# Other digits for how feed-forward pieces and inversion steps are laid between the blocks of an RWKV-7 attention kernel

## The chip, the core and the metric

The kernel runs on one core of a Trainium2 chip: TensorE (in the profile PE for its matmuls and PEld for its weight loads), VectorE (DVE), ScalarE (ACT), GpSimd (POOL), and SyncE (SP), which issues most DMAs. The metric is the device time of one execution in microseconds, and the time of a kernel is the median of its runs.

## The reference: what is computed

```python
# attention, B=4, H=8, S=768, D=40; state is (B, H, D, D)
for t in range(S):
    y[:, :, t] = einsum('bhd,bhde->bhe', rt, state)
    Sa = einsum('bhde,bhe->bhd', state, at)
    state = state * wt[:, :, None, :] - einsum('bhd,bhe->bhde', Sa, bt) \
            + einsum('bhd,bhe->bhde', vt, kt)
x = y.transpose(0, 2, 1, 3).reshape(3072, 320)
# feed-forward, 320 -> 2048 -> 320
h = x @ w_in
out = (h * clip(h + 3, 0, 6) / 6) @ w_out
```

The recurrence over time is sequential; the feed-forward of a token needs only that token's row of `y`.

## The kernel before, in words

**Units.** The attention is cut into chunks of 64 steps. A unit is one chunk of two batches, all heads at once; there are 24 units (`NK`), four (`NU`) to a group of 128 steps. For a unit, `prepare` (L579) does what needs no state: `W` and `gam` (products of the decays, two scans at L599 and L610), `A`, `B`, `K`, `factor` (turning and scaling the inputs), `F` (the products that make up the matrix to invert), `E` and `EV`. `step` (L882) does the rest: `RT` and `VT` (turn), `R` (L921), `C` and `H` (scores, L562, masked on VectorE at L575), `U` and `UT` (L961, L981), `rS` (L997) and `y`, which also updates the state (matmuls L1043, VectorE L1050 and L1055). `move` and `move2` bring `y` into the layout of the feed-forward by DMA.

**Inversion.** Once for a group, when `F` of its last unit is there, `invert` (L778) inverts 32 triangular 32x32 blocks per row of lanes on VectorE: a transpose (L783), then 30 pairs of one multiply (L803) and one add (L809), then two transposes `tb` (L812) and `tt` (L817), then copies to `tinv` on ScalarE and GpSimd. It is a generator: one call of `aside(1)` (L1254) issues the instructions up to its next `yield`. The first call issues the transpose, the second and third nothing, each of the next sixty one multiply or one add, the 64th `tb`, the 65th `tt`. `third_block` (L828) then does the off-diagonal parts on TensorE (L838 and L861, copied out by ScalarE at L846 and L871). It needs `tb` and `tt`.

**Feed-forward.** For each unit there are two jobs. `expand` (L1165) multiplies by 1024 columns of `w_in` into two PSUM banks (`h`, two buffers, both used by each job); when the last product is in, `results` (L1183) takes them out: ScalarE relu (L1186), then VectorE minimum and product (L1187), which frees the banks. `contract` (L1204) multiplies by `w_out` (`o`). `feed_forward` (L1142) runs expand of a job, then contract of the job before it, then expand of the next, and so on: an expand therefore waits until L1187 of the expand before it has run. The stream is a generator too; one `next(stream)` is a *piece*. From unit 7 on, a job has eight pieces: four of expand (four matmuls of 128x128 each) and four of contract (two matmuls with 320 columns each). The eight short matmuls of expand (64 rows, `win2`) are no piece then: they are issued inside the next block's products, and if all four expand pieces are issued by then, `results` follows them at once, else it follows the fourth.

**Order.** The order is written out by hand, engine by engine, as Python emits it; each engine works its list in that order. Units 4 to 23 take four *blocks* each, 80 blocks in all (0 to 79 below, `m` in the code). Block `m` of unit `i` has m = 4(i-4)+j. `a_block(m)` (L1483) issues the stages that fall into that block: those of the unit's own `step` (`RT` and `VT` in its first block, `R`, `C` and `S` in the second, `U`, `UT` and `rS` in the third, `H` in the fourth, `y` in the fifth, so the twenty groups of L1043 stand in blocks 4, 8, ... 80, and the moves in the sixth) and those of the units being prepared ahead. It does so in two parts: the stages of units whose preparation began at a multiple of four blocks with the unit's own, and the stages of the others; after block 14 the second part is always empty. In the first two blocks of the first two units of a group, `block` (L1368) adds the third blocks, L838 in the first of them and L861 in the second. Feed-forward pieces are put between the two parts and after the second part (and the third block) by `feed` (L1506):

```python
def feed(n, inversion):
    for _ in range(n):
        next(stream)
        aside(inversion)
```

with `GAPS` (L1515, pieces per block) and `INVERSION` (L1516, calls of `aside` after each piece of that block), one digit for each block. Before the third block of a group's first unit, `aside(3 * L)` issues what is left of the inversion.

```python
for j in range(BLOCKS):
    amount, inversion = int(GAPS[m]), int(INVERSION[m])
    parts = a_block(m)
    next(parts)                       # first part
    ...                               # first = how many pieces come here
    feed(first, inversion)
    for _ in parts: pass              # second part
    if third_here: ...                # aside(3 * L) once a group, then block(i, j)
    feed(amount - first, inversion)
    m += 1
```

After block 79 the stream runs out whatever is left.

## Time and profile before

| | |
|---|---|
| runs of the kernel before, median | 793.05 us |
| lowest to highest of its 3 runs | 792.87 to 794.69 us |
| the profiled execution | 790.23 us |
| its span in the profile | 788.5 us |
| mean granted TensorE clock in it | 0.954 |
| blocks 0 to 79 | from 194 us on; L1043 of block 16 starts at 314.10 us, of block 32 at 427.60 us, of block 40 at 470.88 us |

The profile shows one execution, a little below the lowest of the three timed runs. In a timeline row the first number is the start in us, the second how long the group was busy, and in brackets stands how long the engine sat idle before it and which instruction ended that. Each fp32 matmul of 128x128 or of 320 columns has two records, so one expand piece is 8 records of L1171 (`h`), one contract piece 4 records of L1212 (`o`), and the short matmuls of a job are 16 records of L1171. In the table of waits stand the engine and line that waited, the line that ended the wait, the sum in us, how often, and the longest.

### The profile page before, as it was taken

Reading aid. Unit: us, or ns where it says so; the run is one execution under the profiler, and the core shown is the slowest. Engines: PE = TensorE matmul, PEld = TensorE weight load, DVE = VectorE, ACT = ScalarE, POOL = GpSimd, SP = SyncE. Lnnn points to the kernel's source line nnn. Section 1 sums busy time; section 2 is a strip of 40 time slices with the busy share of each in tenths; the row PEclk is TensorE's granted clock in tenths of the full one; section 3 lists DMA queues with packets and bytes.
Section 4 is the critical chain, followed back from the end, with each engine's and each line's share of the span. In section 5 each row is a group of like instructions: output and inputs, shape, how many; then the busy total and the mean of one; then the engine's idle time right before and its main releaser. Section 6 shows DMA issues by size and latency. Waiting matters only on the chain.

```text
span 788.5 us, 32736 instructions
## 1 busy us (share of the span) xinstructions
PE 724.5 (92%) x14464; PEld 611.9 (78%) x14464; DVE 508.5 (64%) x1020; ACT 299.0 (38%) x634; POOL 168.2 (21%) x319
## 2 busy tenths in 40 slices
PE   5826888999899997999999999999999999999998
PEld 3725677878778776788888788888888888888886
DVE  8898799688445798555798556997535892233110
ACT  2345673232544442542424454134543233422111
POOL 7503002421222412122203222113222100000000
PEclk9855689999999998999999999999999999999999
DMA  9682384320244421334331344323332201211000
GB/s 124 113 205 62 91 210 75 63 48 12 50 73 76 89 54 27 77 77 90 60 63 36 74 82 87 67 47 68 69 69 57 43 17 38 47 38 29 20 9 17
DMA packets 195698, 52.34 MB, mean 66 GB/s; under 512 B 179428, under 2 KB 194276, under 8 KB 195556
## 3 DMA queue, kind: packets, MB, share of 16 engines
q1 hardware_dynamic: 187932, 46.88, 30.2%
q10 hardware_dynamic: 7624, 3.36, 1.7%
q8 instruction: 114, 1.87, 1.0%
q14 instruction: 28, 0.23, 0.1%
HBM read 38.67 MB, written 3.93 MB: 54 GB/s over the span
## 4 chain that ended last, share of the span: by engine, by line
PE 72%; DVE 15%; issue 4%; ACT 3%; DMA 2%; SPq 1%; POOL 1%; ACTq 1%; DVEq 0%; POOLq 0%
PE h L1171 26%; PE o L1212 23%; PE pair L562 4%; PE pair L1043 3%; DVE prod L803 2%; DVE x L809 2%; PE pair L534 2%; PE pair L961 2%; PE one L524 1%; DVE wm L610 1%; PE pair L997 1%; DVE prods L599 1%; PE pair L861 1%; PE pair L981 1%; PE pair L921 1%
## 5 line engine op out<-in xcount | busy, mean ns | idle before, releaser
L1171 PE MATMUL h<-xt,win 128*128 128x128 f32 (+1 forms) x2304 | 250.2, 284 | 5.9 <-DVE gt L1187 5.8
L1171 PEld LDWEIGHTS h<-xt,win 128*128 128x128 f32 (+1 forms) x2304 | 231.6, 193 | 22.4 <-DVE gt L1187 6.9
L1212 PE MATMUL o<-wout,gt 128*128 128x320 f32 x768 | 228.3, 441 | 0.0
L1212 PEld LDWEIGHTS o<-wout,gt 128*128 128x128 f32 x768 | 138.6, 190 | 51.7
L1187 DVE SCALAR_TENSOR_TENSOR gt<-gt,h 128x512 f32<-128x512 f32 x96 | 61.6, 682 | 105.1 <-ACT gt L1186 105.1
L1186 ACT ACTIVATE gt<-h,three 128x512 f32<-128x512 f32 x96 | 61.4, 684 | 133.1 <-PE h L1171 113.9
L803 DVE TENSOR_TENSOR prod<-x 128x30 f32<-128x30 f32 (+9 forms) x180 | 66.6, 370 | 6.4 <-POOL x L788 1.3
L809 DVE TENSOR_TENSOR x<-x,prod 128x30 f32<-128x30 f32 (+9 forms) x180 | 64.7, 360 | 5.9
L575 DVE COPY_PREDICATED store<-mask,pair 128x512 f32<-128x512 int32 x40 | 29.2, 729 | 54.5 <-PE pair L562 41.0
L1051 POOL TENSOR_TENSOR yg<-ys,gam 128x512 f32<-128x512 f32 x20 | 25.4, 1272 | 150.0 <-DVE ys L1050 145.1
L723 POOL TENSOR_TENSOR KBt<-K,rgt 128x320 f32<-128x320 f32 x19 | 16.7, 881 | 145.5 <-ACT rgt L712 140.3
L599 DVE TENSOR_TENSOR_SCAN prods<-wm,start 128x528 f32<-128x528 f32 x24 | 33.4, 1398 | 11.2 <-ACT wm L596 10.8
L1043 PE MATMUL pair<-store,KBt 64*64 64x104 f32 x1280 | 32.6, 250 | 0.6 <-ACT F L693 0.6
L610 DVE TENSOR_TENSOR_SCAN wm<-wm,start 128x528 f32<-128x528 f32 x24 | 31.0, 1293 | 0.8
L757 ACT ACTIVATE EV<-pair 64x320 f32<-64x320 f32 x46 | 19.8, 431 | 29.9 <-PE pair L752 26.3
L1043 PEld LDWEIGHTS pair<-store,KBt 64*64 64x64 f32 x1280 | 29.2, 133 | 1.5 <-ACT F L693 0.7
L642 POOL TENSOR_TENSOR at<-at,gam 128x512 f32<-128x512 f32 x12 | 15.3, 1271 | 65.8 <-DVE at L478 65.8
L950 ACT ACTIVATE S<-pair 128x512 f32<-128x512 f32 x16 | 9.6, 597 | 47.9 <-DVE store L575 27.1
L871 ACT ACTIVATE tinv<-pair 32x256 f32<-32x256 f32 x48 | 17.9, 374 | 21.4 <-PE pair L861 20.8
L783 DVE STREAM_TRANSPOSE fb<-F 128x1024 f32<-128x1024 f32 x6 | 12.9, 2155 | 18.8 <-ACT F L693 16.8
L1230 ACT ACTIVATE ob<-o 128x320 f32<-128x320 f32 x22 | 9.6, 437 | 40.6 <-issue 25.9
L932 ACT ACTIVATE VT<-pair 128x512 f32<-128x512 f32 x21 | 12.5, 598 | 32.6 <-PE pair L562 18.2
(298 smaller groups left out, 1064.5 us busy)
## 6 DMA issues: line engine op xcount, KB each, us to landing
R<-in_r_dram SPq DMA_DIRECT2D x156, 40.0 KB
A<-in_a_dram SPq DMA_DIRECT2D x61, 80.0 KB
V<-in_v_dram SPq DMA_DIRECT2D x96, 40.0 KB
out_dram<-ob SPq DMA_DIRECT2D x47, 80.0 KB
B<-in_b_dram SPq DMA_DIRECT2D x42, 80.0 KB
store<-V SPq DMA_DIRECT2D x20, 160.0 KB
W<-in_w_dram SPq DMA_DIRECT2D x37, 80.0 KB
K<-in_k_dram SPq DMA_DIRECT2D x37, 80.0 KB
```

Of the source, the lines that this page charges most:

```text
L562: nc.tensor.matmul(out=o[i][half(q), n, :], lhsT=lhs[half(i, D), n ^ (2 * q * swap), half(q)], rhs=rhs[half(i, D), n ^ (2 * q * back), hal ...
L575: nc.vector.copy_predicated(out=x[:, :, 0:BL].rearrange("p (h i) t -> p i h t", i=2), mask=mask8, data=o[2])
L599: nc.vector.tensor_tensor_scan(out=prods[:].rearrange("p r m i -> p (r m i)"), data0=wm[:, 0:SCAN], data1=start[:], initial=0.0, op0=ALU.m ...
L610: nc.vector.tensor_tensor_scan(out=back, data0=back, data1=start[:], initial=0.0, op0=ALU.mult, op1=ALU.add)
L803: nc.vector.tensor_tensor(out=pv, in0=_ap(x[:], (i + 1) * L + i, [[L, n], [0, i]]), in1=_ap(x[:], i * L, [[0, n], [1, i]]), op=ALU.mult,)
L809: nc.vector.tensor_tensor(out=rest, in0=rest, in1=pv, op=ALU.add)
L1043: nc.tensor.matmul(out=y[q][half(s), pr, :], lhsT=o[name][half(q), h * D:h * D + SLOT], rhs=m[name][half(q), x, :], start=(name == "K" and ...
L1051: nc.gpsimd.tensor_tensor(out=yg[:], in0=m["ys"][:].rearrange("p r q t -> p r (q t)"), in1=o["G"][:], op=ALU.mult)
L1171: nc.tensor.matmul(out=hp[c][:, i, :], lhsT=lhsT, rhs=rhs, start=(begun[c] == 0), stop=(begun[c] == 3 * NQ - 1))
L1186: nc.scalar.activation(out=gt[:], in_=hp[c][:], func=AF.Relu, bias=three[:], scale=1.0)
L1187: nc.vector.scalar_tensor_tensor(out=gt[:], in0=gt[:], scalar=6.0, in1=hp[c][:], op0=ALU.min, op1=ALU.mult)
L1212: nc.tensor.matmul(out=op[:], lhsT=gts[c][:, n, :], rhs=wout[:, c * HJ + r * NQ + n, :], start=((split or r == 0) and c == 0 and n == 0), ...
```

## The change

Three strings of digits. `GAPS` and `INVERSION` get other digits; a third string, `FIRSTS`, gives for each block how many of its pieces come between the two parts, where before it was half of them in blocks that have a third block or a stage in the second part, and none otherwise. The first digit of `GAPS` that differs is that of block 3, and the first digit of `INVERSION` that differs while an inversion is open is that of block 12, in unit 7, where the group of units 8 to 11 is inverted.

```diff
-    GAPS = "71052314311277562421243135343899422124213525759654324442543253966531154234264363"
-    INVERSION = "00000000000034230000000000221223000000000012232300000000001323230000000000122343"
+    GAPS = "71042423221267761421243135344795544114204515859744312732442443878512353433263353"
+    FIRSTS = "50021102120130201200121000200000210032022200010022104300003011113420021202121001"
+    INVERSION = "01210000000015231100000000231231000001000012142300111011000324230000000001203323"
...
-            ahead_here = any(begin % BLOCKS and m - begin < len(order) and order[m - begin]
-                             for (u, begin), (_, order) in ahead.items())
-            first = amount // 2 if third_here or ahead_here else 0
+            first = min(amount, int(FIRSTS[m]))
             feed(first, inversion)
```

The sum of `GAPS` goes from 301 to 300. The number and kind of instructions on each engine stay the same. In the order in which the two programs hand them out, these are the differences around blocks 3 to 40 (b is the place between the parts, e the place after them, h an expand piece, o a contract piece, s a step of the inversion, "short" the short matmuls in the block's own products):

| block | before | after |
|---|---|---|
| 0 | b ooo, e o hhh | b oooo h, e hh |
| 3 | b short o, e ooo | b short o, e oo |
| 5 | b o, e o | b o, e oo |
| 6 | e h | e hh |
| 7 | b hh, e h short | b hh, e short |
| 8 | b h, e hh | b h, e h |
| 9 | e h | b hh |
| 12 | b oo h, 6 s; e hhh o, 12 s | b oo h; e hhh, 3 s |
| 13 | e ooo hhhh, 28 s | e oooo hhh, 35 s |
| 14 | short with results; b oo, 4 s; e oo h, 6 s | short; b h with results, o, 4 s; e ooo hh, 10 s |
| 15 | short; e hhh with results, ooo, 4 s, `tb`, `tt` before results | short; e hh with results, oooo, 8 s, `tb`, `tt` after results |
| 16 | b o, e h | b h |
| 27 | e ooo h, 8 s | e ooo h, 12 s |
| 28, 29 | e hhh; e oooo hhhh, 16 s | e hhh o; e ooo hhhh, 14 s |
| 30 | short with results; e oooo hhhh o, 18 s | the same, 27 s |
| 31 | short with results; e ooo hhhh oo, 12 s, `tb`, `tt` | short with results; e ooo hh, `tb`, `tt` |
| 32 to 34 | b oo, e hh; b h, e h; e oo | b hh, e ooo; b o, e hhh; e h ooo |
| 39, 40 | e o; e hhh | none; b o h, e hh |

From block 41 on the digits differ by 1 to 3 in about half of the blocks. Over all blocks the stream is at no place more than four pieces behind or two ahead of where it was.

## The prediction

> **What bounds the kernel now.** First the page: how long TensorE is busy, and at which clock.

> ```profile
> span 788.5 us, 32736 instructions
> PE 724.5 (92%) x14464; PEld 611.9 (78%) x14464; DVE 508.5 (64%) x1020; ACT 299.0 (38%) x634; POOL 168.2 (21%) x319
> ```

> TensorE is the bound, with 64 us of its span idle. An average over stages does not say where, so the busy time by stretches comes next (columns: length, then busy time of PE, PEld, DVE, ACT, POOL, then the granted clock).

> ```profile
> 250.00:300.00 50.00, 43.72 (x872) 36.20 (x864) 37.54 (x82) 19.92 (x48) 12.73 (x25) 1.00 0.36 70
> 300.00:350.00 50.00, 48.14 (x1136) 40.96 (x1140) 33.23 (x64) 20.88 (x46) 13.57 (x22) 0.93 0.32 64
> 350.00:400.00 50.00, 48.70 (x966) 41.73 (x958) 32.80 (x64) 17.93 (x41) 13.02 (x25) 1.00 0.37 75
> 400.00:450.00 50.00, 49.66 (x1040) 41.94 (x1042) 37.19 (x78) 22.35 (x49) 9.57 (x15) 1.00 0.26 53
> 450.00:500.00 50.00, 49.47 (x1167) 42.03 (x1160) 31.57 (x61) 21.57 (x52) 14.53 (x28) 1.00 0.40 80
> 500.00:600.00 100.00, 100.00 (x2021) 85.45 (x2020) 68.93 (x139) 38.17 (x84) 21.02 (x37) 1.00 0.32 65
> 600.00:700.00 100.00, 99.86 (x1980) 84.13 (x1979) 56.00 (x118) 34.28 (x70) 13.46 (x25) 1.00 0.18 38
> ```

> From 400 to 700 us TensorE idles for 0.34 + 0.53 + 0 + 0.14 = 1.0 us. Whatever the digits do in those blocks (29 to 70 or so), there is 1 us to win, and only new waits to lose. From 250 to 400 us it idles for 6.3 + 1.9 + 1.3 us. The table of waits from block 0 to the end says for whom.

> ```profile
> PE h L1171 <- DVE gt L1187: 4.5, 1, 4.5
> PE pair L861 <- DVE wm L646: 1.3, 1, 1.3
> PE pair L997 <- DVE score L571: 1.3, 1, 1.3
> PE pair L683 <- ACT ys L1003: 1.2, 1, 1.2
> PE pair L997 <- ACT tinv L871: 0.4, 1, 0.4
> PE pair L961 <- ACT F L693: 0.4, 1, 0.4
> ```

> One wait towers over the rest: an expand that cannot begin since VectorE has not taken out the expand before. Its place is block 14, and the inversion of units 8 to 11 is its cause. VectorE, in order of time (`prod` and `x` are the inversion's steps):

> ```profile
> 296.70 0.39 DVE L803 TENSOR_TENSOR prod<-x 128x220 f32<-128x220 f32 x1
> ...
> 299.83 1.28 DVE L1187 SCALAR_TENSOR_TENSOR gt<-gt,h 128x512 f32<-128x512 f32 x2
> ...
> 304.00 0.25 DVE L809 TENSOR_TENSOR x<-x,prod 128x84 f32<-128x84 f32 x1
> 306.79 0.69 DVE L738 TENSOR_TENSOR kt<-pair,rgam 128x512 f32<-128x512 f32 x1 [2.54 <-PE pair L534]
> ...
> 314.56 0.44 DVE L908 TENSOR_TENSOR state<-state,scale 128x320 f32<-128x320 f32 x1
> 315.78 0.69 DVE L1050 TENSOR_TENSOR ys<-pair,ys 128x512 f32<-128x512 f32 x1 [0.77 <-PE pair L1043]
> 316.39 0.98 DVE L1055 TENSOR_TENSOR state<-pair,state 40x320 f32<-40x320 f32 x2
> ```

> The take-out at 299.83 stands in VectorE's list behind all 28 steps of block 13. TensorE in the same time:

> ```profile
> 293.60 2.42 PE L1212 MATMUL o<-wout,gt 128*128 128x320 f32 x8
> 300.56 4.08 PE L1171 MATMUL h<-xt,win 128*128 128x128 f32 x24 [4.54 <-DVE gt L1187]
> ...
> 306.65 2.94 PE L1171 MATMUL h<-xt,win 128*128 128x128 f32 x24
> 309.43 3.40 PE L1212 MATMUL o<-wout,gt 128*128 128x320 f32 x12
> 312.66 0.60 PE L524 MATMUL one<-ident,W 128*128 128x128 f32 x4
> ...
> 315.64 1.34 PE L1212 MATMUL o<-wout,gt 128*128 128x320 f32 x4
> 317.51 0.74 PE L838 MATMUL pair<-tb,F 32*32 32x32 f32 x64 [0.53 <-DVE state L1055]
> 318.19 2.25 PE L1171 MATMUL h<-xt,win 128*128 128x128 f32 x24
> ```

> TensorE runs dry at 296.02. And the wait costs more than itself, as the granted clock shows:

> ```profile
> 207.60:211.00 3.40, 3.40 (x40) 2.95 (x38) 0.77 (x2) 1.45 (x4) 0.00 (x0) 0.50 0.27 48
> 299.70:306.60 6.90, 6.04 (x72) 5.55 (x72) 4.24 (x13) 0.00 (x0) 0.00 (x0) 0.51 0.01 2
> ```

> After the wait TensorE runs at half clock for 6.9 us, so VectorE in turn stands for 2.54 us until TensorE has turned `K` for it. The two engines hold each other up, one after the other.

> **The change part by part.** The instructions are the same before and after, in number and kind; only their order moves. No DMA is added, and none that I see late: in the trace no engine but ScalarE waits for one in blocks 12 to 16.

> *Blocks 12 to 17.* Steps leave block 12 (18 become 3) and come to blocks 13 to 15. One piece fewer comes before block 14, so the expand ends there in the first piece, and its take-out is issued behind 3 + 35 steps instead of 6 + 12 + 28 = 46. Eight steps go behind it: those from 296.70 to 299.83, 3.13 us. So the take-out starts at about 296.7, and TensorE, which got going 0.73 us after its start (300.56 - 299.83), begins at 297.4. The contraction still ends at about 296.0: up to the expand that waits, both orders have handed out 44 pieces. The wait falls from 4.54 to about 1.4 us.

> That is not yet the gain, since VectorE's list is the same work up to the state update of block 16 (316.39 + 0.98 = 317.37), and L838 waits for that update. Its two waits for TensorE in that stretch, 2.54 and 0.77 us, go if TensorE is early enough: at full clock it does, after 297.4, two pieces and the short matmuls (2.25 + 0.98; 24 records of pieces took 2.94, so one is 0.98), then L703, L562 and L534 (304.44 to 306.65 is 2.2 us at half clock, so 1.1), ending at 301.7, when VectorE still has steps of block 14; then two pieces (1.96), four contract pieces (3.40 / 3 x 4 = 4.53) and L524 to L1043 (312.66 to 315.64, 2.98), so L1043 ends at 311.2. VectorE without its two waits reaches the state update at 317.37 - 3.31 = 314.06. TensorE now puts the expand piece of block 16 ahead of L838 (until 312.1) and waits 2 us there, with L838 at 314.2 instead of 317.51. Behind L838 nothing is left of block 16, where 0.98 us followed before. **Gain 3.3 + 1.0 = 4.3 us.** If VectorE did not bound it, the most would be 3.1 of the wait and half of 6.9 us at half clock, 6.6 us. From below it is what the new wait at L838 can cost: if it too lowers the clock, half of one stretch of 3.40 us, 1.7 us.

> [...]

> *Blocks 3 and 5.* A contract piece goes from block 3, where TensorE runs without a wait, to block 5, behind L861. There stand two waits:

> ```profile
> 235.03 0.68 PE L961 MATMUL pair<-RR,tinv 64*64 64x40 f32 x32 [0.39 <-ACT F L693]
> 236.59 0.69 PE L997 MATMUL pair<-RT,S 40*64 40x64 f32 x32 [0.40 <-ACT tinv L871]
> ```

> Both end on ScalarE's list, which starts with block 5 and so comes earlier with it. The piece (3.40 / 3 = 1.13 us) covers both: **0.8 us** (0 if VectorE is late in block 4, 1.1 at most).

> *Blocks 8 and 9.* A piece goes from block 8 to block 9, ahead of the second part. L997 of block 10 waits 1.31 us for the mask behind `prods`, behind ScalarE's copy of `W`:

> ```profile
> 253.71 0.66 PE L524 MATMUL one<-ident,W 128*128 128x128 f32 x4
> 255.85 0.39 ACT L592 ACTIVATE wm<-one 128x256 f32<-128x256 f32 x1 [2.20 <-DMA xt<-yg]
> 258.48 0.69 PE L997 MATMUL pair<-RT,S 40*64 40x64 f32 x32 [1.31 <-DVE score L571]
> ```

> ScalarE is held until 255.85 by issuing the four moves of block 9. They come a piece (0.98) earlier now, so ScalarE is free at 254.9. The products of `W` (253.71) come the same piece earlier and two pieces later, 253.71 - 0.98 + 1.96 = 254.7, and are done 0.5 later: the copy starts at 255.2, 0.65 earlier, and L997 with it. **0.6 us** (0 to 1.0).

> *Blocks 26 to 34.* Steps are drawn together into block 30 (18 become 27), and four pieces leave block 31 for blocks 32 to 34. The take-out at the start of block 31 then has twelve more steps ahead of it:

> ```profile
> 413.80 0.33 DVE L809 TENSOR_TENSOR x<-x,prod 128x168 f32<-128x168 f32 x1
> 415.42 1.28 DVE L1187 SCALAR_TENSOR_TENSOR gt<-gt,h 128x512 f32<-128x512 f32 x2 [1.28 <-ACT gt L1186]
> 416.16 3.50 PE L1212 MATMUL o<-wout,gt 128*128 128x320 f32 x12
> ```

> They are the last and shortest, no longer than 0.33 us with a gap of 0.03: 12 x 0.36 = 4.3 us at most, of which 1.28 fits in VectorE's idle time. So the take-out starts at 418.4 at the latest and frees the first bank 0.73 us after; the expand that needs it comes after the contract pieces, 416.16 + 3.40 = 419.6. No cost, with half a microsecond to spare. The four pieces are paid one for one where they go.

> *All blocks after 34.* Block 39 has no piece left: `y` of block 40 then comes 1.1 us earlier than its mask, for about 0.4 us, and in block 34 the added piece covers about as much. The rest lies where TensorE has no idle time: 0, from -1.0 (all that is there) to +1.0.

> The sum: 4.3 + 0.8 + 0.6 = 5.7 us. On the profiled execution, 790.23 us (span 788.5), this gives 784.5. It lies 2.8 us under the median of the runs, 793.05; the difference carried over to the median gives **787.4 us**.

> **The rivals.** *The clock is lowered again* at the 2 us wait at L838, or at the 1.4 us before it: 1.7 us a time, 789.1 or, twice, 790.8. For it speaks the stretch at 207.60; against it that the wait of 1.3 us at L997 (258.48) left it at 1.00 from 250 to 300 us. *Nothing moves*: VectorE finds in its list no shorter way to block 16 (its two waits return elsewhere, behind `kt` or the copies of ScalarE), and the early pieces only change places; 793.0. The two rows of its waits speak against it. That most new digits of `INVERSION` stand where no inversion is open, and those of `FIRSTS` where there is no second part, makes the change smaller than it looks, but not in block 12 to 15. *It ends slower*: blocks 9, 16, 36, 39, 52, 58 and 66 end without a piece, as block 2 does before, where L683 waited 1.2 us for ScalarE. Seven such waits of 1.3 us are 9.1 us, 3.4 more than the gain: 796.5. It decides from 0.8 us a block. Against it: in all but block 39 pieces stand earlier in the same block, with at most the second part or L838 behind them, so that what the next block reads has that time; I take 0.4 for block 39 and nothing for the others. *It gains more*: VectorE is not the bound at L838, 6.6 in place of 4.3: 785.1.

> **How the numbers follow.** The forecast with its small terms either way (785.5 to 789.0) has 0.56, more gain 0.08, the lowered clock 0.17, nothing 0.12, slower 0.07. About 0.3%, 2.4 us, is what a measurement of this kernel can tell from no change: faster 0.81, same 0.12, slower 0.07. The range reaches from the larger gain with the 1.0 us of the late blocks (784.1) to no change with its noise (793.4).

> **What would show it.** In the profile after: the wait of L1171 for L1187 near 296 is 1 to 2 us, not 4.5; VectorE does not wait for L534 in block 15; L838 of block 16 waits about 2 us for L1055 and starts 3 us or more ahead of its place; the granted clock from 300 to 350 us is above 0.93; L961 and L997 of block 6 wait for nothing; L997 of block 10 for about 1 us. From 400 us on TensorE idles for no more than 2 us. The prediction fails if the first take-out of block 14 still stands behind steps for 4 us, if the late blocks show waits of over 4 us together, or if L838 waits for over 4 us.

## The result and the profile after

The changed kernel takes 788.87 us in the median of 7 runs (786.03 to 790.08), the kernel before, on the same chip, 794.16 us (7 runs, 790.2 to 795.54). The ratio is 0.9944, with a 95% interval from 0.9916 to 0.9971. Two more comparisons came with the experiments below: 0.9946 (0.9923 to 0.9969) and 0.9955 (0.9932 to 0.9979). By these ratios the gain is 3.6 to 4.4 us. A single run of the experiments below (800.51 us, at a mean clock of 0.906) was slow and is left out of the ratios and medians. The profiled execution took 786.03 us, against 790.23 before.

First the head of the page. TensorE has the same number of instructions as before and is busy with them for 6.9 us less.

```profile
span 784.3 us, 32739 instructions
PE 717.6 (91%) x14464; PEld 607.4 (77%) x14464; DVE 507.6 (65%) x1020; ACT 299.6 (38%) x634; POOL 168.6 (21%) x319
```

Then the busy time by stretches (columns as before):

```profile
250.00:300.00 50.00, 47.25 (x941) 39.90 (x940) 39.95 (x89) 18.45 (x44) 12.52 (x25) 1.00 0.35 68
300.00:350.00 50.00, 46.63 (x1160) 39.52 (x1159) 30.59 (x57) 24.53 (x56) 13.82 (x22) 0.97 0.35 71
350.00:400.00 50.00, 48.18 (x1002) 41.41 (x999) 38.10 (x78) 17.04 (x38) 12.99 (x25) 1.00 0.37 74
400.00:450.00 50.00, 48.92 (x1008) 40.91 (x1006) 35.22 (x71) 21.68 (x49) 12.35 (x20) 1.00 0.28 56
450.00:500.00 50.00, 48.72 (x1061) 41.72 (x1062) 32.16 (x63) 19.59 (x46) 13.02 (x26) 1.00 0.41 82
500.00:600.00 100.00, 99.91 (x2124) 85.07 (x2123) 66.26 (x133) 41.89 (x93) 20.76 (x34) 1.00 0.31 63
600.00:700.00 100.00, 100.00 (x1875) 84.07 (x1873) 53.45 (x115) 31.44 (x62) 12.54 (x23) 1.00 0.17 37
```

From 250 to 300 us TensorE idles for 2.8 us instead of 6.3; from 300 to 350 us it idles for 3.4 instead of 1.9. A wait has moved. The table of waits, from block 0 on, says where to:

```profile
PE pair L838 <- DVE state L1055: 4.1, 3, 2.7
PE pair L861 <- DVE wm L646: 1.3, 1, 1.3
PE pair L683 <- ACT ys L1003: 1.2, 1, 1.2
PE pair L997 <- DVE score L571: 1.1, 1, 1.1
PE h L1171 <- DVE gt L1187: 1.1, 1, 1.1
PE pair L534 <- ACT rgt L712: 0.9, 1, 0.9
```

The 4.5 us of the expand are 1.1 us now, and L838 waits instead. TensorE and VectorE around both places:

```profile
294.50 3.14 PE L1171 MATMUL h<-xt,win 128*128 128x128 f32 x32 [1.10 <-DVE gt L1187]
311.82 0.86 PE L838 MATMUL pair<-tb,F 32*32 32x32 f32 x64 [2.66 <-DVE state L1055]
```

```profile
272.50 2.15 DVE L783 STREAM_TRANSPOSE fb<-F 128x1024 f32<-128x1024 f32 x1
293.76 1.28 DVE L1187 SCALAR_TENSOR_TENSOR gt<-gt,h 128x512 f32<-128x512 f32 x2
300.17 0.68 DVE L738 TENSOR_TENSOR kt<-pair,rgam 128x512 f32<-128x512 f32 x1
302.63 1.28 DVE L1187 SCALAR_TENSOR_TENSOR gt<-gt,h 128x512 f32<-128x512 f32 x2 [0.41 <-ACT gt L1186]
310.09 0.68 DVE L1050 TENSOR_TENSOR ys<-pair,ys 128x512 f32<-128x512 f32 x1
310.69 0.98 DVE L1055 TENSOR_TENSOR state<-pair,state 40x320 f32<-40x320 f32 x2
```

L738 and L1050 have no bracket any more: VectorE waits for TensorE at neither place. From the transpose that opens the inversion (272.50) to the state update (310.69) it takes 38.2 us. Before, these two instructions stood 41.9 us apart:

```profile
274.49 2.15 DVE L783 STREAM_TRANSPOSE fb<-F 128x1024 f32<-128x1024 f32 x1
```

to 316.39. This distance is the measure used below, since it doesn't depend on how long the start-up took. Besides the two waits for TensorE, VectorE has lost a third one, for GpSimd, which stood right behind the transpose in the kernel before:

```profile
277.25 0.20 DVE L803 TENSOR_TENSOR prod<-x 128x30 f32<-128x30 f32 x1 [0.61 <-POOL x L788]
```

In the changed kernel a mask (L571) stands there in VectorE's list, ahead of the inversion's first step, and fills the wait. The granted clock, in the stretch that holds the wait at L838 and the one after it:

```profile
308.80:312.30 3.50, 0.84 (x58) 0.68 (x60) 3.41 (x8) 1.92 (x5) 2.54 (x4) 0.99 0.22 51
312.30:315.70 3.40, 3.40 (x69) 3.22 (x61) 3.28 (x7) 1.61 (x5) 0.89 (x3) 0.50 0.43 91
```

So L838 pays twice: 2.66 us of wait, and 3.4 us at half clock behind it.

A second distance shows what TensorE gains by all this: from the start of L1043 in block 12 to its start in block 20. In between, both kernels work off the same 34 pieces. It is 68.29 us before (267.49 to 335.77) and 64.72 us in this profile of the change (265.48 to 330.20).

### The profile page after: what moved, and what is told of

Read it like the earlier page. It is cut to its first block, busy times and chain, and to the rows that moved or that the text cites. A ratio compares the mean times of both kernels' runs of the same rounds, so it can differ in the third digit from the quotient of the medians.

```text
span 784.3 us, 32739 instructions
## 1 busy us (share of the span) xinstructions
PE 717.6 (91%) x14464; PEld 607.4 (77%) x14464; DVE 507.6 (65%) x1020; ACT 299.6 (38%) x634; POOL 168.6 (21%) x319
## 4 chain that ended last, share of the span: by engine, by line
PE 72%; DVE 14%; ACT 4%; issue 3%; DMA 3%; SPq 2%; POOL 1%; ACTq 0%; DVEq 0%; POOLq 0%
PE h L1171 25%; PE o L1212 23%; PE pair L562 4%; PE pair L1043 3%; DVE prod L803 2%; DVE x L809 2%; PE pair L534 2%; PE pair L961 1%; PE one L524 1%; PE pair L921 1%; DVE prods L599 1%; PE pair L981 1%; PE pair L861 1%; PE pair L997 1%; PE pair L838 1%
## 5 line engine op out<-in xcount | busy, mean ns | idle before, releaser
L1171 PE MATMUL h<-xt,win 128*128 128x128 f32 (+1 forms) x2304 | 249.5, 283 | 3.8 <-DVE gt L1187 3.0
L1171 PEld LDWEIGHTS h<-xt,win 128*128 128x128 f32 (+1 forms) x2304 | 231.3, 192 | 19.7 <-DVE gt L1187 3.6
L1212 PE MATMUL o<-wout,gt 128*128 128x320 f32 x768 | 227.3, 441 | 0.0
L1212 PEld LDWEIGHTS o<-wout,gt 128*128 128x128 f32 x768 | 138.9, 190 | 51.6
L1187 DVE SCALAR_TENSOR_TENSOR gt<-gt,h 128x512 f32<-128x512 f32 x96 | 61.8, 682 | 100.9 <-ACT gt L1186 99.8
L1186 ACT ACTIVATE gt<-h,three 128x512 f32<-128x512 f32 x96 | 61.9, 684 | 120.5 <-PE h L1171 100.3
L803 DVE TENSOR_TENSOR prod<-x 128x30 f32<-128x30 f32 (+9 forms) x180 | 65.2, 362 | 6.5 <-POOL x L788 1.3
L809 DVE TENSOR_TENSOR x<-x,prod 128x30 f32<-128x30 f32 (+9 forms) x180 | 64.6, 359 | 5.8
L1043 PE MATMUL pair<-store,KBt 64*64 64x104 f32 x1280 | 32.6, 250 | 0.7 <-ACT F L693 0.5
L1043 PEld LDWEIGHTS pair<-store,KBt 64*64 64x64 f32 x1280 | 29.2, 133 | 1.4 <-ACT F L693 0.7
L738 DVE TENSOR_TENSOR kt<-pair,rgam 128x512 f32<-128x512 f32 x14 | 9.6, 685 | 29.0 <-PE pair L703 28.6
L965 ACT ACTIVATE store<-pair 128x320 f32<-128x320 f32 x23 | 10.0, 436 | 41.7 <-PE pair L981 31.2
L871 ACT ACTIVATE tinv<-pair 32x256 f32<-32x256 f32 x48 | 17.9, 373 | 15.8 <-PE pair L861 12.7
```

The source lines that it names most:

```text
L803: nc.vector.tensor_tensor(out=pv, in0=_ap(x[:], (i + 1) * L + i, [[L, n], [0, i]]), in1=_ap(x[:], i * L, [[0, n], [1, i]]), op=ALU.mult,)
L809: nc.vector.tensor_tensor(out=rest, in0=rest, in1=pv, op=ALU.add)
L1043: nc.tensor.matmul(out=y[q][half(s), pr, :], lhsT=o[name][half(q), h * D:h * D + SLOT], rhs=m[name][half(q), x, :], start=(name == "K" and ...
L1171: nc.tensor.matmul(out=hp[c][:, i, :], lhsT=lhsT, rhs=rhs, start=(begun[c] == 0), stop=(begun[c] == 3 * NQ - 1))
L1186: nc.scalar.activation(out=gt[:], in_=hp[c][:], func=AF.Relu, bias=three[:], scale=1.0)
L1187: nc.vector.scalar_tensor_tensor(out=gt[:], in0=gt[:], scalar=6.0, in1=hp[c][:], op0=ALU.min, op1=ALU.mult)
```

## The experiments

Two questions stood open. Which half of the change shortens VectorE's list (the time from L783 to L1055 above), the pieces or the steps? And what does the wait at L838 cost? The theory is that of the prediction: VectorE bounds blocks 12 to 16, and the change takes away its waits for TensorE. The rivals are that the blocks outside 12 to 16 bring the gain, or that the clock takes it back.

**Blocks 12 to 16 alone.** The kernel before with the new digits of these five blocks only:

```diff
-GAPS[12:17], FIRSTS[12:17], INVERSION[12:17] = "77562", "30201", "34230"
+GAPS[12:17], FIRSTS[12:17], INVERSION[12:17] = "67761", "30201", "15231"
```

> The digits of blocks 12 to 16 alone are new, everything else as before. Theory (VectorE's list in the inversion of units 8 to 11 carries the gain): the waits of these blocks are those of the changed kernel, about 1.1 us of L1171 for L1187 and 2.7 us of L838 for L1055, the wait of VectorE for L534 in block 15 is gone; 3 us of the time go, 3.5 if the clock stays up at L838 (ratio to before 0.995 to 0.997). Rival (the gain comes from blocks 0 to 11 and from where a half-clock stretch happens to fall there): the time is that of before within 1 us, whatever the two waits do. Second rival (L838 only takes over the wait): TensorE reaches block 17 less than 1 us earlier than before, counted from block 12.

Measured: 0.9980 (0.9958 to 1.0002), less than the 0.995 to 0.997 expected. The waits are those of the changed kernel, 1.1 us at L1171 and 2.61 us at L838, and the 38.2 us of VectorE too. Behind L838 the clock stayed low for 10.2 us:

```profile
308.00:311.40 3.40, 0.99 (x8) 0.80 (x8) 3.30 (x7) 2.50 (x5) 2.57 (x5) 1.00 0.12 28
311.40:321.60 10.20, 10.00 (x216) 9.55 (x220) 6.50 (x13) 2.10 (x5) 2.73 (x6) 0.50 0.42 91
```

The clock granted there is 0.50; half of 10.2 us, an estimate of the loss, is 5.1 us, more than the 3.7 us won ahead of it. From L1043 of block 12 to L1043 of block 20 this execution takes 67.50 us, barely less than with the old digits (68.29 in the profile before, 67.69 in each of the next two runs). Once, at 470 us, L1043 also waited 2.0 us for a DMA.

**All but blocks 12 to 16.** The changed kernel with the old digits of these five blocks (the diff above the other way round):

> The changed kernel with the digits of before in blocks 12 to 16. Theory: the 4.5 us wait of L1171 for L1187 is back with half clock behind it, and L838 of block 16 waits 0.5 us; of the 5.3 us of the change about 2 are left (blocks 5 to 10), less about 2 for new waits after block 28, so the time is within 1.5 us of before (ratio 0.998 to 1.001). Rival (blocks 0 to 11): the time stays 4 us or more below before.

Measured: 0.9984 (0.9961 to 1.0007), as expected; the wait at L1171 is back (4.6 us), VectorE takes 41.3 us.

**Blocks 0 to 11 alone.** The digits of `INVERSION` for blocks 1 to 3 are new too; no inversion is open there.

```diff
-GAPS[0:12], FIRSTS[0:12] = "710523143112", "300211021001"
+GAPS[0:12], FIRSTS[0:12] = "710424232212", "500211021201"
```

> The digits of blocks 0 to 11 alone are new. Theory: L961 and L997 of block 6 wait for nothing (0.8 us before), L997 of block 10 waits 1.1 instead of 1.3 us; counted from block 3 to block 11, TensorE is 1.2 to 1.6 us earlier than before; ratio 0.998 to 0.999, too small for the runs to tell. Rival (the early pieces only change places): no gain from block 3 to block 11. Rival (they carry the change): ratio 0.995.

Measured: 0.9989 (0.9966 to 1.0011). The waits of L961 and L997 of block 6 (0.4 us each) are gone from the table of waits; L997 of block 10 still waits:

```profile
PE h L1171 <- DVE gt L1187: 4.6, 1, 4.6
PE pair L997 <- DVE score L571: 1.3, 1, 1.3
```

Each of these three intervals contains 1, so they rank nothing by themselves: neither blocks 12 to 16 alone nor the rest alone shows the whole gain. The traces tell more. From L861 of block 1 to L1043 of block 12 the pieces are the same in all kernels. With half clock near 207 us, that stretch takes 60.83 to 60.89 us with the old digits (three profiles) and 59.19 to 59.54 with the new ones (eight); without it, 59.60 (one profile) and 57.70 to 57.83 (two). So blocks 2 to 11 gain 1.3 to 1.9 us, a third to a half of the whole, much as the expectation for blocks 0 to 11 had it (1.2 to 1.6).

**Steps alone and pieces alone.** Only the steps of blocks 12 to 16 are new, everything else as before:

```diff
-INVERSION[12:17] = "34230"
+INVERSION[12:17] = "15231"
```

> Only the inversion's digits of blocks 12 to 15 are new; the pieces stand as before. 39 steps stand ahead of the take-out of block 14 instead of 46. Theory (the steps ahead of the take-out set the wait): seven steps of 0.39 us, 2.7 us less, so L1171 waits 1.8 us instead of 4.5 (0.7 of it is the take-out's own first half), VectorE's wait for L534 in block 15 is gone, and the gain is 2.5 to 3.5 us (ratio 0.996 to 0.997). Rival (the piece moved out of block 12, with the end of the expand in block 14, makes the gain): the wait stays above 3.5 us and the time within 1 us of before.

Only the pieces are new, everything else as before:

```diff
-GAPS[12:17] = "77562"
+GAPS[12:17] = "67761"
```

> Only the pieces of blocks 12 to 16 and their split are new; the inversion steps of these blocks and all other blocks are as in the kernel before. It is the complement of the run with only the steps new. Theory, that the wait for the take-out L1187 goes by the steps set ahead of it, and the pieces only move where TensorE runs ahead: the wait at L1171 falls from 4.6 us to about 3.3 us by the shifted pieces alone, the half clock behind it stays (3 to 7 us of it), L838 of block 16 waits about 1 us, and the time is that of the kernel before within 0.3 per cent. Rival, that pieces alone bring the gain of 3 to 4 us: the wait at L1171 is under 2 us and the time 0.995 to 0.996 of the kernel before.

Measured: the steps alone 1.0025 (1.0006 to 1.0044), slower than before; the pieces alone 0.9978 (0.9958 to 0.9998). The expectation for the steps missed: they were to be faster and came out slower. That for the pieces had the time within 0.3 per cent of the kernel before, as it is, but the wait of the expand was to be 3.3 us and was 2.3. Waits of TensorE, the steps alone first, then the pieces alone:

```profile
PE pair L838 <- DVE state L1055: 4.3, 3, 3.1
PE h L1171 <- DVE gt L1187: 2.3, 1, 2.3
```

```profile
PE h L1171 <- DVE gt L1187: 2.3, 1, 2.3
PE pair L838 <- DVE state L1055: 2.0, 3, 0.7
```

Each half takes about 2.2 us off the wait at L1171. VectorE's list takes 40.4 us with the steps and 40.6 us with the pieces (with the old digits 41.9 in the profile before and 41.3 in the two runs above; together 38.2). So each half shortens it by about a third of what both do. What sets the two apart is L838. With the pieces it waits 0.7 us, and no half clock follows. With the steps, where one piece fewer stands ahead of it (56 instead of 57), it waits 3.06 us, and 6.8 us at half clock follow:

```profile
315.80:322.60 6.80, 6.40 (x124) 6.03 (x128) 4.38 (x8) 1.92 (x5) 1.60 (x4) 0.50 0.41 83
```

A list shorter by 0.9 to 1.5 us, less half of 6.8 us for the clock, makes by estimate 1.9 to 2.5 us slower, 1.0024 to 1.0032; measured 1.0025. From L1043 of block 12 to L1043 of block 20 the steps alone take 69.24 us, 1.0 to 1.6 more than the old digits, and the pieces alone 66.25, 1.4 to 2.0 less. The half clock of the kernel before lies ahead of L838, and what it costs there is part of VectorE's list (the 2.54 us for L534); behind L838 it comes on top.

**The late blocks taken back.** The changed kernel with the old digits from block 31 on; from the end of block 30 on, the order is that of the kernel before.

```diff
-GAPS[31:] = "5544114204515859744312732442443878512353433263353"
+GAPS[31:] = "9422124213525759654324442543253966531154234264363"
-FIRSTS[31:] = "0210032022200010022104300003011113420021202121001"
+FIRSTS[31:] = "0210012000000000022002200000000003200020000000000"
-INVERSION[31:] = "1000001000012142300111011000324230000000001203323"
+INVERSION[31:] = "3000000000012232300000000001323230000000000122343"
```

> The changed kernel in blocks 0 to 30, and the digits of the kernel before in blocks 31 to 79. Theory, that the digits from block 31 on give nothing and cost the small waits that the changed kernel shows in blocks 37, 40, 43, 53 and 66: these go, block 34 has its wait of about 0.4 us again, and the time is 1 to 2.5 us below the changed kernel, 0.997 to 0.999 of it. Rival, that these waits are filled slack and the sum of matmuls alone sets the time from 400 us on: as the changed kernel within 0.1 per cent.

Measured: 0.9955 (0.9933 to 0.9977), median 789.25 us, and the changed kernel beside it 789.29. The waits of blocks 37, 40 and 43 are gone, but L534 waits 0.8 us for the DMA of `B` instead, and the time shows no gain. For 2 us a comparison of this spread is too coarse; that the late digits lose 1 to 2.5 us is not shown.

**Pieces ahead of L838.** The decisive series changes how long L838 waits, and nothing ahead of that. One expand piece fewer in block 16, one more, and two more, each given to or taken from block 25:

```diff
-GAPS[16], FIRSTS[16], GAPS[25] = 1, 1, 5
+GAPS[16], FIRSTS[16], GAPS[25] = 0, 0, 6      # one piece fewer
+GAPS[16], FIRSTS[16], GAPS[25] = 2, 2, 4      # one more
+GAPS[16], FIRSTS[16], GAPS[25] = 3, 3, 3      # two more
```

Two more, run twice (the first expectation calls them contract pieces; where they fall, they are expand pieces):

> The changed kernel with two more feed-forward pieces ahead of the matmuls L838 in block 16 (taken from after the inversion of block 25). Theory, that TensorE is 2.7 us ahead of VectorE there and the wait with the half clock behind it is what eats part of the gain: two contract pieces are 8 records of 0.2 us, 1.7 us; the wait at L838 falls from 2.66 us to about 1 us, no stretch at half clock follows it, and the kernel takes 2 to 4 us less than the changed one, about 0.995 to 0.997 of it, 0.989 to 0.992 of the kernel before. Rival, that VectorE's work bounds blocks 14 to 17 whatever TensorE is given: the wait goes but comes back as a wait of 1 to 2 us at L861 or L838 of blocks 17 to 18 or in blocks 25 to 30, where the pieces are taken from, and the time is that of the changed kernel within 0.2 per cent.

> The kernel with two expand pieces more ahead of L838 in block 16 again, for a narrower interval beside the two others of the series and for the length of its later waits. Theory: no stretch at half clock behind L838 again, wait 0.8 to 0.9 us, and the time 1.5 to 4 us below the changed kernel, 0.989 to 0.993 of the kernel before. Rival, that its first median was low by the luck of seven runs, and the gain is only the 0.4 us that the loop of its profile shows: 0.994 of the kernel before.

One fewer, one more, and the changed kernel beside them and beside the first run of two more:

> The changed kernel without the expand piece ahead of L838 in block 16 (given to block 25). The suspected wait made longer: by the theory that VectorE fixes the start of L838, the wait is 3.5 to 3.6 us, and at half clock 6.8 or 10.2 us follow; 0.9 us for the piece and 1.7 us for each stretch of 3.4 us more, so 2.5 to 4.3 us slower than the changed kernel, 1.003 to 1.005 of it. Rival, that the piece only waits with it and VectorE is not the bound (TensorE itself starts L838 earlier without the piece): the wait stays below 3 us and the time is that of the changed kernel within 0.1 per cent.

> The changed kernel with one expand piece more ahead of L838 in block 16 (taken from block 25). Three earlier numbers bear on it: with the pieces of the changed kernel the wait at L838 was 2.61 to 2.66 us with 3.4 or 6.8 us at half clock behind it, with two pieces more it was 0.85 us with none. Theory, that VectorE fixes the start of L838 and a piece of 0.92 us fills the wait: the wait is 1.7 to 1.8 us. Theory, that the clock is judged in stretches of 3.41 us, and that a stretch busy for less than about 0.4 is followed by one at half clock while one busy for 0.62 or more is not, or not always: a wait of 1.75 us leaves a stretch busy for at least 0.49, so in the profiled execution most likely no stretch at half clock follows. Then 1.5 to 2.5 us less than the changed kernel, 0.997 to 0.998 of it. Rival, that any wait above 1.3 us lowers the clock: a stretch of 3.4 us at half clock follows and the time is that of the changed kernel less 0.9 us.

> The changed kernel itself beside the others on the same chip, so that differences of 0.2 per cent between them can be told. By its first comparison 0.992 to 0.997 of the kernel before. Theory, that the half clock behind the wait at L838 differs in length between executions of one kernel: the wait is again 2.6 to 2.8 us, and the stretch behind it 3.4, 6.8 or 10.2 us long, with the time 0, 1.7 or 3.4 us longer. Rival, that the stretch is fixed by the kernel: 3.4 us at 312 us from the start again.

> The changed kernel beside the series of one piece less, one more and two more, as its middle point on the same chip. By its two comparisons 0.9945 of the kernel before; wait at L838 2.6 us, with one or two stretches of 3.4 us at half clock behind it. Theory of the stretches: whether the 1.3 us wait near 207 us is followed by half clock differs between executions, while the wait at L838 always is. Rival: the half clock behind L838 is absent in this one.

| pieces ahead of L838 | wait at L838 | at half clock behind it | L1043, block 12 to 28 | median | ratio to before |
|---|---|---|---|---|---|
| 0 | 3.72 us | 6.8 us | 118.19 us | 791.46 us | 0.9983 (0.9959 to 1.0008) |
| 1 (the change), second run | 2.61 us | 6.8 us | 117.41 us | 789.29 us | 0.9946 (0.9923 to 0.9969) |
| 1 (the change), third run | 2.61 us | 6.8 us | 116.44 us | 790.64 us | 0.9955 (0.9932 to 0.9979) |
| 2 | 1.74 us | 6.8 us | 116.33 us | 787.52 us | 0.9920 (0.9892 to 0.9948) |
| 3, first run | 0.85 us | none | 113.57 us | 785.50 us | 0.9912 (0.9882 to 0.9943) |
| 3, second run | 0.85 us | none | 112.84 us | 786.04 us | 0.9915 (0.9887 to 0.9942) |

The wait, the half clock and the distance are those of the one profiled execution of each. The distance runs from the start of L1043 in block 12 to its start in block 28; block 25 lies inside it, so TensorE works off the same 59 pieces in every row. The first profile of the change, with 3.4 us at half clock, has 114.68 us, the profile before 118.74. So the length of the half clock behind one and the same wait is not fixed by the kernel. L838 with no piece, with one (third run) and with three (first run) ahead of it, in executions in which the inversion's transpose L783 starts at the same time (276.42, 276.33 and 276.37 us):

```profile
315.70 0.74 PE L838 MATMUL pair<-tb,F 32*32 32x32 f32 x64 [3.72 <-DVE state L1055]
```

```profile
315.61 0.74 PE L838 MATMUL pair<-tb,F 32*32 32x32 f32 x64 [2.61 <-DVE state L1055]
```

```profile
315.65 0.74 PE L838 MATMUL pair<-tb,F 32*32 32x32 f32 x64 [0.85 <-DVE state L1055]
```

L838 starts at the same time, whatever TensorE is given to do ahead of it: VectorE fixes its start (its list takes 38.2 us in all of them). A piece put there is done for nothing, 0.9 us each (1.1 for the first). The clock decides the rest. The stretch of 3.4 us that holds the wait, and what follows, with one piece (third run), two pieces, and three (second run):

```profile
313.80:317.20 3.40, 1.59 (x80) 1.58 (x80) 3.33 (x6) 1.47 (x5) 1.52 (x3) 1.00 0.36 79
317.20:324.00 6.80, 6.48 (x101) 6.03 (x98) 4.76 (x11) 1.35 (x4) 2.00 (x4) 0.50 0.41 85
```

```profile
310.80:314.20 3.40, 1.66 (x79) 1.45 (x79) 3.35 (x5) 1.47 (x5) 1.65 (x2) 1.00 0.34 76
314.20:321.00 6.80, 6.64 (x102) 6.18 (x99) 5.48 (x12) 2.21 (x5) 1.87 (x4) 0.50 0.40 82
```

```profile
309.50:312.90 3.40, 2.55 (x82) 2.35 (x82) 3.23 (x7) 1.51 (x5) 2.15 (x4) 1.00 0.26 60
312.90:316.30 3.40, 2.96 (x97) 2.68 (x98) 3.28 (x8) 2.09 (x5) 0.90 (x3) 1.00 0.45 89
```

TensorE busy for 1.59 or 1.66 us of 3.4: half clock follows. Busy for 2.55 us: it stays at full clock. With three pieces two pieces of 0.9 us are filled in and 3.4 us (half of 6.8) are saved, by estimate 5.2 us, against an execution of the change with 6.8 us at half clock; the distances in the table differ by 2.9 to 4.6 us. The medians differ by 3.8 (785.50 against 789.29) and 4.6 us (786.04 against 790.64), the ratios by 2.7 and 3.2 us, and new waits, such as 0.45 us of L534 behind L838, take part of the difference. The expectation for two pieces named full clock as the most likely, and the profile has half clock; its time, 3.1 us under the change where a piece alone gives 0.9, would fit executions without it, but the interval doesn't exclude 0.9. With no piece ahead, the ratio is 2.2 us above that of the third run of the change, just under the 2.5 to 4.3 us expected; the intervals don't tell this from 0.9 us, the piece alone. The rival, a wait below 3 us, is ruled out by the 3.72. L534 behind L838 also waits 1.54 us there, by a cause that the profile doesn't show.

The kernel with three pieces there beats both others: about 0.9 per cent below the kernel before, 0.3 to 0.4 below the change. Its interval overlaps that of the change in each comparison; that both comparisons and the distances agree is what carries it.

## Why the prediction came out as it did

787.4 us was forecast, a gain of 5.7 us. The medians of the first comparison differ by 5.3 us, those of the two others by 3.9 and 2.8, and the ratios of all three say 3.6 to 4.4. That the first comes so close to 5.7 is in part luck: the sum had no term for the clock. Step by step:

- **The wait of the expand.** Forecast about 1.4 us, measured 1.10. Right, and each half of the change brings half of it.
- **VectorE's two waits.** Both are gone, and its list is shorter by 3.1 to 3.7 us (41.3 or 41.9 to 38.2); forecast 3.3. Right, but the size is partly luck. The wait of 0.61 us for GpSimd behind the transpose also went, which the forecast didn't see, and a new one of 0.41 us, for ScalarE's relu at 302.63, came: 2.54 + 0.77 + 0.61 - 0.41 = 3.5, and the remaining 0.2 is in the instructions' own time.
- **L838 of block 16.** Forecast: it waits 2 us, measured 2.61 to 2.66. The place and the cause are right, the series shows that VectorE sets its start, and the gain of this stage without the clock, 3.1 to 3.7 and the piece of 0.9 us, is near the 4.3 forecast.
- **The clock behind L838.** Here the forecast erred. Its sum takes the wait of 2 us to cost no clock, and no run shows that: in all three profiles of the change the wait, 2.61 to 2.66 us, is followed by half clock, for 3.4, 6.8 and 6.8 us; half of that, 1.7 to 3.4 us, is the estimate of what it costs. The rival that had 0.17 is what happens. From L1043 of block 12 to L1043 of block 20, executions with the new digits of blocks 12 to 16 take 64.72 and 65.22 us with one stretch of 3.4 us, 66.41 and 66.55 with two, and 67.50 with three, against 67.69 to 68.29 with the old digits. So one stretch leaves 2.5 to 3.6 us of the 4.3, two leave 1.1 to 1.9, and three 0.2 to 0.8. Half clock also came without a stretch in which TensorE stood still throughout: with one piece more it followed a stretch of 3.40 us (from 310.80 us) with 1.66 us of work.
- **The clock near 207 us.** It wasn't in the sum. Before had 3.4 us at half clock there, the change in its profile has none, though L861 waits 1.31 us in both. That is worth 1.5 us, of the 4.2 by which the two profiled executions differ: from L861 of block 1 to L1043 of block 4 the first profile of the change takes 12.59 us, its second 14.10. The second and third runs of the change have it again (at 211.1 and 211.4 us), and the run of the steps alone, with the old digits there, has none. It isn't the change's doing. Here is the first profile of the change:

```profile
207.60:211.00 3.40, 3.22 (x124) 2.97 (x128) 1.94 (x5) 1.50 (x4) 0.00 (x0) 1.00 0.39 69
```

- **Blocks 3 and 5.** The two waits, 0.8 us together, are gone, as forecast. **Blocks 8 and 9**: L997 of block 10 was to wait about 1 us and waits 1.11 us in the first profile, 1.3 in the run of blocks 0 to 11 alone, against 1.31 before. Of the 0.6 us, 0 to 0.2 is shown as a shorter wait. By the distance to L1043 of block 12, though, blocks 2 to 11 together gain 1.3 to 1.9 us, where 0.8 + 0.6 = 1.4 was forecast.

```profile
256.47 0.69 PE L997 MATMUL pair<-RT,S 40*64 40x64 f32 x32 [1.11 <-DVE score L571]
```

- **Late blocks.** From 400 to 700 us TensorE idles for 1.08 + 1.28 + 0.09 + 0 = 2.45 us; the limit named was 2. Block 40 waits twice the forecast 0.4, and ahead of that stretch block 29, whose cost was put at nothing, waits 1.37 us instead of 0.73:

```profile
387.74 0.69 PE L562 MATMUL pair<-RT,VT 40*64 40x64 f32 x32 [1.37 <-DVE start L608]
464.46 0.46 PE L534 MATMUL pair<-ident,V 64*128 64x64 f32 x8 [0.87 <-ACT rgt L712]
```

Block 29 differs between executions (0.72 us in the second run of the change); block 40 waits about 0.9 us in all three. A loss is not shown by this, however. The profile before shows the old late digits at their best: the five other executions that have them wait 0.6 to 3.1 us in all for DMAs between 455 and 485 us, the one before doesn't. From L1043 of block 28 to the end the old digits of blocks 31 to 79 take 402.3 to 407.8 us (six profiles), the new ones 403.3 to 405.2 (eight).

Put together by distances: blocks 2 to 11 gain 1.3 to 1.9 us. From L1043 of block 12 to that of block 28 the change takes 114.68 us with one stretch at half clock behind L838, and 116.44 and 117.41 with two, against 117.90 to 118.74 with the old digits of blocks 12 to 16 (three profiles): a gain of 3.2 to 4.1, or of 0.5 to 2.3. From block 28 on neither a gain nor a loss is shown. That makes 4.5 to 6.0 us with one stretch and 1.8 to 4.2 with two; the ratios, 3.6 to 4.4, lie within that. How often an execution has one stretch and how often two is not known from three profiles, so the split stays open.

## What to carry to other kernels

When a wait is removed, ask which engine sets the next meeting point, and compute where the faster engine will now stand idle, and give it independent work just there: here L838 started at 315.70 us with no piece ahead of it, at 315.61 with one and at 315.65 with three. Ask also what that idle time does to the clock (here 3.4 to 10.2 us at half clock stood behind a wait of 2.6 us), and whether the half clock then falls where TensorE is the bound. Judge such a change by distances inside the loop between two points with the same work, since single executions of one kernel differ by more than the change is worth (785.32 to 793.93 us in 12 runs of the change, for a gain of 3.6 to 4.4 us).

## What the hardware showed

Back at full clock took one to three such stretches: 3.4, 6.8 and 10.2 us behind the same wait of 2.6 us. Where half clock held for one stretch, TensorE had no gap in it: 3.40 us of work in 3.40 at 207.6 us before, at 312.3 us in the first profile of the change, at 298.7 us with the steps alone, at 302.4 us with the pieces alone. Where it held for longer there were gaps: 6.04 us of work in 6.90 (299.7 us before), 5.26 to 6.75 in 6.80 (behind L838, with the steps alone and in the series), 10.00 in 10.20 (blocks 12 to 16 alone). That this is a rule is not shown.

Executions of one kernel also differ by 3.8 us at block 16 already, more than the change is worth in most of its parts. In the changed kernel, the same L838 with the same wait starts at 311.82 us in the first profile and at 315.61 us in the third. Of that, 2.2 us are there at L861 of block 1 (207.78 and 209.96 us), and 1.5 come from the half clock right behind it. 12 runs of the change in one comparison lie between 785.32 and 793.93 us.
